# Own buffers for scaled weights, a key block's scores moved, transposes grouped, a last store in halves

## The chip, the cores and the metric

The kernel runs on one core of a Trainium2 chip. The metric is the time of one execution on the device in microseconds, taken as the median of several runs; lower is better.

## The reference

Three parts follow each other, all in fp32: attention over 4 x 12 heads of 448 tokens and 64 columns (scores capped by a tanh, softmax), a gated layer with two matmuls behind it, and a SoLU layer with a norm and a last matmul.

```python
scores = cap * np.tanh(scale * np.matmul(q, k.transpose(0, 1, 3, 2)) / cap)
attn = np.exp(scores - max); attn = attn / (attn.sum(-1) + 1e-09)
x = (attn @ v).transpose(0, 2, 1, 3).reshape(1792, 768)
h = ((x @ w1) * (x @ w2)) @ w3 @ w_out          # (1792, 768)
h = h @ w_in                                    # (1792, 1024)
solu = h * softmax(h)
ln = (solu - mean(solu)) / np.sqrt(var(solu) + 1e-06) * g_ln
out = ln @ moe2_w_out                           # (1792, 768)
```

(`max`, `mean` and `var` go along the last axis.) All weights come in as float64 and are turned into fp32 on the chip.

## The kernel before, in words

Every large product is made of three matmuls on operands split into a high and a low fp32r part (`THREE`). The kernel has these stages.

**Attention with the fold beside it** (0 to about 435 us). 24 pairs of heads are worked on in 12 groups `g` of three phases. Keys are cut in four chunks: three full ones for each head of the pair, and a fourth, the last keys, in which both heads' last 64 keys lie together. `scores` (L237 to L251) writes the scores of a chunk to a PSUM tile `sc0` or `sc1` (two banks each), `exps` (L257, L258) runs tanh in place and then exp to `p` on ScalarE, `split_scores` (L269 to L273) makes `hi` and `lo`, and `values` (L290) sums into the banks `o`. The first four pairs (`PLAIN`) skip the split of the scores. Beside this, `fold` multiplies w3 by w_out (L378) and the result by w_in (L396), once for all tokens, in two PSUM banks of tag `f`. From about 270 us on the gated products `ab` (L604) run beside the last heads, with `a` copied by ScalarE (L608) and `abs` multiplied on VectorE (L612).

**The queue of weights.** `Ahead` holds a list of pieces to be loaded, converted and split; `step` does the `rest` of the piece before and the `first` of the next. Loads go three ahead into `ld` (tag `ld`, 3 buffers, L159 or L161). `convert` turns a float64 piece into fp32 with three VectorE instructions (L168 to L170) in a buffer of tag `cv` (2 buffers). For most weights `split` then reads it (ScalarE L174, VectorE L175). For the last weights (`plan_last`, L529) ScalarE multiplies the `cv` buffer in place by g_ln (L535), and SyncE stores it to `wg_dr` (L536); 16 such pieces are stored between 359 and 467 us, the last four of them after the attention.

**The gated products alone** (about 435 to 580 us): `products` takes two PSUM tiles per weight block and batch, 36 matmuls into the two. Beside it `plan_sums` (L494 to L497) makes sums and differences of weight quarters in tiles `t` (tag `ts`) and stores them (L499).

**Seven-product blocks** (580 us to the end): 14 blocks, seven for the first matrix and seven for the last, each of seven products of 12 matmuls (L766) for a 2 x 2 block scheme. `seven` (L761) runs products 1, 2, 6, 7, 5, 4, 3; `kept` copies three of the partial sums from PSUM to SBUF (`p1`, `u2`, `p7`; L770), and VectorE adds them (L777, L786, L789); product 6 goes on in the bank that `p1` was copied from. The last part is copied by ScalarE (L791). Between the blocks `solu` does the row-wise part and stores it to `c_dr`; `turned` (L831) transposes the loaded tiles on TensorE (L836) into four banks `tp`, a quarter each time that `seven` calls `other`. The results go out in stores of 128 x 768 (L903).

**Order.** The program's instructions are put in order on each engine at build time, by a schedule that works with priorities and estimated times; `tc.high_priority` and `tc.issue_after` steer it. At run time each engine works strictly in its order.

**The start.** `load_pair(0)` loads q, k and v of the first pair (L197, L202), then `ahead.loads()` the first three weight pieces. 12 products of a zero tile (L663) run ahead of the first scores, and six more (L701) behind the scores of chunk 1. `ready[0]` takes pair 0 unsplit.

Of the kernel before, what the change touches and what calls it, by code (L numbers as in the profile page):

```python
# [38 lines left out]
WARM = 12  # L39
# [11 lines left out]
class Ahead:  # L51
# [9 lines left out]
    def loads(self):  # L61
        while self.loaded < len(self.items) and self.loaded < self.at + self.depth:
            _, load, _, _, _, there = self.items[self.loaded]
            if there is not None and not there():
                return
            load()
            self.loaded += 1

# [30 lines left out]
def attention_moe_solu(ctx: ExitStack, tc: tile.TileContext, q, k, v, cap, w12, w3t, wo, win, wout2, g_ln, out):  # L99
# [89 lines left out]
    def load_pair(n):  # L189
# [6 lines left out]
        for t, src in ((qd, q), (kd, k)):  # L196
            sync.dma_start(out=t, in_=src[n])  # L197
        if n in PLAIN:
            vd = at.tile([P, 2, S], F32, tag="lo", bufs=4, name=f"vf{n}").rearrange("p a b -> p (a b)")
            vd = vd[:, :NV * (D + 1)].rearrange("p (c d) -> p c d", c=NV)  # L200
            pool.memset(vd[:, :, D:], 1.0)
            sync.dma_start(out=vd[:, :, :D], in_=v[n])  # L202
        else:
            vd = at.tile([P, NV, D], F32, tag="vd", name=f"vd{n}")
            sync.dma_start(out=vd, in_=v[n])
# [31 lines left out]
    def scores(n, c, place_):  # L237

        qh, ql, kh, kl = ready[n][:4]
        sc = ps.tile([P, 2, HALF], F32, tag=f"sc{place_}", name=f"sc{n}_{c}")  # L240
# [246 lines left out]
    def plan_sums(kind, dr, t_dr, i_, part, n):  # L487
# [3 lines left out]
        def rest():  # L491
            b = lands.pop(i).rearrange("p (g h n) -> p g h n", g=2, h=2)
            t = [place["ts"].tile([P, HALF], F32, tag="ts", bufs=6, name=f"t{i}_{m}")[:, :2 * n].rearrange("p (t n) -> p t n", t=2) for m in range(2)]
# [35 lines left out]
    def plan_last(f):  # L529
        for u in range(2):  # L530
            i = len(ahead.items)

            def rest(i=i, u=u):
                t = cvs.pop(i)
                act.activation(t, t, AF.Copy, scale=gt[:, f:f + 1])  # L535
                sync.dma_start(out=wg_dr[f, u], in_=t)  # L536
            ahead.add(("g", f, u), lambda i=i, u=u: landing(i, wout2[f, u].bitcast(U32), DM, U32), lambda i=i: convert(i, DM // 2), rest)
# [118 lines left out]
    load_pair(0)  # L656
# [32 lines left out]
    for g in range(NP // 2):  # L689
        n, first, at_once = 2 * g, g % 2, 2 * g in PLAIN  # L690
        for phase in range(3):
# [6 lines left out]
            if not g and not phase:  # L698
                with tc.issue_after(tiled[0].ins):
                    for i in range(WARM // 2):  # L700
                        pe.matmul(idle[:, :S], zero[:, 0, :P], zero[:, 0], start=True, stop=True)  # L701
# [6 lines left out]
            for turn, x in enumerate((run[0], (n + phase, 3), run[1])):  # L708
                if turn == 1:
                    if phase == 2:  # L710
                        continue
                    with tc.high_priority():
                        sc = scores(*x, one)
                else:
                    sc = tiles[turn // 2]
# [45 lines left out]
    def seven(n, a, wb, w, c1, c2, other):  # L761
# [6 lines left out]
        def kept(bank, name):  # L768
            t = hp.tile([P, HALF], F32, tag="kept", bufs=3, name=f"{name}_{n}")[:, :w]
# [21 lines left out]
        act.copy(c1[:, w:], u)  # L791
# [39 lines left out]
    def turned(n, tps, q):  # L831

        tps[q] = ps.tile([P, HALF], F32, tag="tp", bufs=4, name=f"tp{n}_{q}")
        for i in range(4):
            f = 4 * (q // 2) + i
            pe.transpose(tps[q][:, i * P:(i + 1) * P], lands[f"c{2 * n + q % 2}"][:, f * P:(f + 1) * P], ident)  # L836
# [41 lines left out]
    for n in range(PAIRS):  # L878
# [4 lines left out]
        seven(n, a, ws, HALF, h1, h2, lambda q: turned(0, tps, q) if last else None)  # L883
# [14 lines left out]
    for n in range(PAIRS):  # L898
        tps, last = {}, n + 1 == PAIRS
        o1, o2 = (hp.tile([P, DF], F32, tag="h", bufs=4, name=f"o{t}")[:, :DM] for t in (2 * n, 2 * n + 1))  # L900
        seven(PAIRS + n, a, wg, w, o1, o2, lambda q: None if last else turned(n + 1, tps, q))
        for t, o in ((2 * n + 1, o2), (2 * n, o1)):
            sync.dma_start(out=out[t * P:(t + 1) * P, :], in_=o)  # L903
# [60 lines left out]
```

## Time and profile before

| | us |
|---|---|
| median of 3 runs | 836.03 |
| lowest, highest | 836.0, 838.24 |
| the profiled execution, its own time | 837.27 |
| its span, first to last instruction | 835.5 |
| TensorE busy with matmuls (PE) | 819.0 |
| VectorE (DVE) busy | 586.2 |
| ScalarE (ACT) busy | 478.4 |

A profile shows one execution. PE is TensorE's matmuls, PEld its weight loads, DVE is VectorE, ACT ScalarE, POOL GpSimd, SP SyncE, which issues most DMAs. L604 is line 604 of the kernel. An instruction's names are "out<-in". A wait is the idle time of an engine before an instruction, with what ended it. The ends of matmuls are modelled, so busy time of PE contains overlap.

### The profile page before, as it was taken

What the parts mean: (1) busy time and instruction counts of PE and PEld (TensorE: products, weight loads), DVE (VectorE), ACT (ScalarE), POOL (GpSimd) and SP (SyncE); (2) the same over time, 40 slices, a digit from 0 to 9 for tenths busy, and PEclk for the clock granted to TensorE, in tenths of its full rate; (3) what the DMA queues carried; (4) which work ended last, traced back from release to release, by engine and by line L of the source; (5) the groups of instructions that cost most, each with busy time, mean ns of one, the idle gap of its engine ahead of it and who ended that gap; (6) DMA issues with size and microseconds to landing.
All of it is one profiled execution on the core that took longest, in us unless ns stands there. A gap on an engine that the chain in (4) does not pass through costs nothing.

```text
span 835.5 us, 12215 instructions
## 1 busy us (share of the span) xinstructions
PE 819.0 (98%) x4363; PEld 682.9 (82%) x4363; DVE 586.2 (70%) x1048; ACT 478.4 (57%) x739; POOL 74.8 (9%) x149
## 2 busy tenths in 40 slices
PE   8999999999999999999899999999999999999998
PEld 4657888866777888887779899998888888999997
DVE  6889968878875787778855452433987877995452
ACT  6767868778677877765752220212555656763341
POOL 1110110110311221111111000000000000000000
PEclk9999999999999999999999999999999999999999
DMA  7878645578977355688677999983533325844211
GB/s 239 273 240 275 209 150 157 175 222 280 277 263 206 114 183 184 207 269 274 198 232 259 347 381 346 360 287 102 184 113 115 100 101 186 264 156 152 89 64 75
DMA packets 95645, 173.48 MB, mean 208 GB/s; under 512 B 13280, under 2 KB 66272, under 8 KB 93536
## 3 DMA queue, kind: packets, MB, share of 16 engines
q1 hardware_dynamic: 90592, 161.51, 57.5%
q0 software_dynamic: 4992, 11.19, 5.4%
q8 instruction: 34, 0.56, 0.3%
q14 instruction: 27, 0.22, 0.1%
HBM read 116.40 MB, written 50.68 MB: 200 GB/s over the span
## 4 chain that ended last, share of the span: by engine, by line
PE 70%; DVE 11%; DMA 11%; ACT 4%; issue 3%; SPq 0%; POOL 0%; DVEq 0%; POOLq 0%; ACTq 0%
PE ab L604 20%; PE u L766 16%; PE v L766 8%; PE o L290 6%; PE f L396 6%; PE f L378 5%; PE y L766 4%; DMA wg_dr<-cv 3%; PE sc L249 3%; DVE cv L169 2%; DMA ld<-in_wo 2%; DVE cv L170 2%; PE tp L836 1%; DVE cv L168 1%; DVE lo L273 1%
## 5 line engine op out<-in xcount | busy, mean ns | idle before, releaser
L604 PE MATMUL ab<-xs,wt 128*128 128x448 f32 x1152 | 241.7, 366 | 2.5 <-DVE abs L612 1.6
L604 PEld LDWEIGHTS ab<-xs,wt 128*128 128x128 f32 x1152 | 216.0, 188 | 23.9 <-DVE abs L612 2.0
L257 ACT ACTIVATE sc<-sc,qscale 128x896 f32<-128x896 f32 (+1 forms) x96 | 84.9, 884 | 34.8 <-PE sc L249 26.4
L258 ACT ACTIVATE p<-sc,capt 128x896 f32<-128x896 f32 (+1 forms) x96 | 85.6, 916 | 1.5
L290 PE MATMUL o<-hi,v 128*66 128x448 f32 (+1 forms) x360 | 84.7, 371 | 0.8 <-ACT x L306 0.6
L766 PE MATMUL u<-ws,a 128*128 128x512 f32 x336 | 82.1, 394 | 0.0
L378 PEld LDWEIGHTS f<-w,w_o 128*128 128x128 f32 x576 | 72.7, 191 | 10.5 <-issue 5.9
L378 PE MATMUL f<-w,w_o 128*128 128x256 f32 x576 | 78.5, 289 | 1.4 <-DVE w_o L175 0.9
L766 PEld LDWEIGHTS u<-ws,a 128*128 128x128 f32 x336 | 62.8, 187 | 14.8
L273 DVE TENSOR_TENSOR lo<-p,hi 128x896 fp32r<-128x896 f32 x60 | 64.9, 1084 | 9.7 <-ACT hi L269 9.5
L396 PE MATMUL f<-w_i,w 128*128 128x512 f32 x288 | 70.2, 393 | 1.1 <-DVE w L175 0.8
L608 ACT COPY a<-ab 128x448 f32<-128x448 f32 x32 | 17.0, 532 | 88.4 <-PE ab L604 84.1
L766 PE MATMUL u<-wg,c 128*128 128x384 f32 x336 | 65.4, 340 | 0.0
L396 PEld LDWEIGHTS f<-w_i,w 128*128 128x128 f32 x288 | 53.7, 188 | 14.3 <-DVE w L175 1.2
L168 DVE TENSOR_SCALAR cv<-ld 128x512 uint32<-128x512 uint32 (+1 forms) x80 | 32.8, 413 | 41.8 <-DMA wg_dr<-cv 25.3
L290 PEld LDWEIGHTS o<-hi,v 128*66 128x66 f32 (+1 forms) x360 | 39.1, 135 | 26.1 <-issue 9.1
L766 PEld LDWEIGHTS u<-wg,c 128*128 128x128 f32 x336 | 58.3, 188 | 0.1
L269 ACT CAST hi<-p 128x896 fp32r<-128x896 f32 x60 | 56.6, 947 | 0.4
L612 DVE TENSOR_TENSOR abs<-ab,a 128x448 f32<-128x448 f32 x32 | 19.9, 621 | 48.5 <-PE ab L604 41.3
L169 DVE SCALAR_TENSOR_TENSOR cv<-ld,cv 128x512 uint32<-128x512 uint32 (+1 forms) x80 | 52.1, 659 | 0.8
L170 DVE SCALAR_TENSOR_TENSOR cv<-ld,cv 128x512 uint32<-128x512 uint32 (+1 forms) x80 | 52.1, 658 | 0.7
L290 PE MATMUL o<-lo,v 128*66 128x448 f32 x120 | 42.6, 367 | 2.4 <-DVE lo L273 2.3
(132 smaller groups left out, 1237.4 us busy)
## 6 DMA issues: line engine op xcount, KB each, us to landing
ld<-in_w SPq DMA_DIRECT2D x24, 512.0 KB, 4.3
w_dr<-wt SPq DMA_DIRECT2D x8, 1536.0 KB, 6.5
wt<-w_dr SPq DMA_DIRECT2D x8, 1536.0 KB, 8.8
ld<-in_w3t SPq DMA_DIRECT2D x16, 512.0 KB, 4.4
ab_dr<-abs SPq DMA_DIRECT2D x32, 224.0 KB, 4.9
ldab<-ab_dr SPq DMA_DIRECT2D x14, 512.0 KB, 3.9
c_dr<-e SPq DMA_DIRECT2D x14, 512.0 KB, 2.6
ldc<-c_dr SPq DMA_DIRECT2D x14, 512.0 KB, 3.6
```

The source lines that it names most:

```text
L168: dve.tensor_scalar(x, hi, 5, 2, ALU.logical_shift_left, ALU.logical_shift_right)
L169: dve.scalar_tensor_tensor(x, hi, 0xC0000000, x, ALU.bitwise_and, ALU.bitwise_or)
L170: dve.scalar_tensor_tensor(x, lo, 29, x, ALU.logical_shift_right, ALU.bitwise_or)
L257: act.activation(sc[:, :w, :S], sc[:, :w, :S], AF.Tanh, scale=qscale)
L258: exp_[n, c] = act.activation(p, sc[:, :w, :S], AF.Exp, scale=capt)
L269: act.copy(hi, p)
L273: dve.tensor_tensor(lo, p, raw(hi), ALU.subtract)
L290: product_.append(pe.matmul(outs[n, j][:v_.shape[-1], :S], v_, t[rows, j if c < 3 else 0], **flags))
L378: pe.matmul(f[:, :QW], lw[:, a], rw[:, e], start=(g == 0 and m == 0), stop=(g == NF - 1 and m == 2))
L396: pe.matmul(f, w34[:, a, c, :], rw[:, e], start=(c == 0 and m == 0), stop=(c == NC - 1 and m == 2))
L604: pe.matmul(pp[f, b, i][:, :S], w[:, u], xs[b, c][:, e], start=(c == 0 and m == 0), stop=(c == NC - 1 and m == 2))
L766: pe.matmul(bank, a[m][:, x, k * P:(k + 1) * P], wb[m][:, e, k, :], start=(first and k == 0 and i == 0), stop=(k == NF // 2 - 1 and i == 2 ...
```

## The change

- `plan_last`: the scaled piece goes to a tile of its own, tag `wg`, 2 buffers; `cv` is no longer written in place. To make room, `ts` has 5 buffers for 6 and `kept` 2 for 3.
- Start: ten zero products, all ahead of the first scores; none behind them. The first weight load is issued between the loads of k and v of pair 0. In the first phase the scores of the last keys go to a bank of tag `f`, and their turn (exp and values) comes after chunk 1.
- `seven` calls `other` once, after product 6, and `turned` then does all 16 transposes.
- The last block: the last copy is shared by ScalarE and VectorE, and each result tile is stored in two halves.

```diff
@@ constants @@
-WARM = 12
+WARM = 10
@@ class Ahead @@
+    def first(self):
+        self.items[0][1]()
+        self.loaded = 1
@@ load_pair @@
-    def load_pair(n):
+    def load_pair(n, between=lambda: None):
         for t, src in ((qd, q), (kd, k)):
             sync.dma_start(out=t, in_=src[n])
+        between()
@@ scores @@
-        sc = ps.tile([P, 2, HALF], F32, tag=f"sc{place_}", name=f"sc{n}_{c}")
+        if place_ is None:
+            sc = ps.tile([P, HALF], F32, tag="f", bufs=2, name=f"sc{n}_{c}").rearrange("p (a s) -> p a s", a=1)
+        else:
+            sc = ps.tile([P, 2, HALF], F32, tag=f"sc{place_}", name=f"sc{n}_{c}")
@@ plan_sums: tag="ts" @@
-bufs=6
+bufs=5
@@ plan_last @@
-                t = cvs.pop(i)
-                act.activation(t, t, AF.Copy, scale=gt[:, f:f + 1])
+                t = conv.tile([P, DM // 2], F32, tag="wg", bufs=2, name=f"wg{f}_{u}")
+                act.activation(t, cvs.pop(i), AF.Copy, scale=gt[:, f:f + 1])
                 sync.dma_start(out=wg_dr[f, u], in_=t)
@@ start @@
-    load_pair(0)
+    load_pair(0, ahead.first)
@@ phases @@
-            if not g and not phase:
-                with tc.issue_after(tiled[0].ins):
-                    for i in range(WARM // 2):
-                        pe.matmul(idle[:, :S], zero[:, 0, :P], zero[:, 0], start=True, stop=True)
-            for turn, x in enumerate((run[0], (n + phase, 3), run[1])):
-                if turn == 1:
-                    if phase == 2:
-                        continue
-                    with tc.high_priority():
-                        sc = scores(*x, one)
-                else:
-                    sc = tiles[turn // 2]
+            turns = [(run[0], tiles[0]), ((n + phase, 3), None), (run[1], tiles[1])]
+            if phase == 2:
+                turns.pop(1)
+            elif not g and not phase:
+                turns[1:] = turns[:0:-1]
+            for x, sc in turns:
+                if sc is None:
+                    with tc.high_priority(), tc.issue_after(tiled[0].ins) if not (g or phase) else nullcontext():
+                        sc = scores(*x, one if g or phase else None)
                 split_scores(*x, exps(*x, sc))
@@ seven: tag="kept" @@
-bufs=3
+bufs=2
@@ seven @@
         dve.tensor_tensor(c1[:, :w], y, p1, ALU.add)
-        other(0)
         product(u, 6, False)
         u2 = kept(u, "u2")
-        other(1)
+        other()
         product(v, 7, True)
         p7 = kept(v, "p7")
-        other(2)
         product(u, 5, False)
         dve.tensor_tensor(c2[:, w:], u, p7, ALU.add)
-        other(3)
...
-        act.copy(c1[:, w:], u)
+        if last:
+            act.copy(c1[:, w:w + w // 2], u[:, :w // 2])
+            dve.tensor_copy(c1[:, w + w // 2:], u[:, w // 2:])
+        else:
+            act.copy(c1[:, w:], u)
@@ turned @@
-    def turned(n, tps, q):
+    def turned(n, tps):
+        for q in range(4):
...
@@ last blocks @@
-            sync.dma_start(out=out[t * P:(t + 1) * P, :], in_=o)
+            for part in (slice(0, w), slice(w, DM)) if last else (slice(0, DM),):
+                sync.dma_start(out=out[t * P:(t + 1) * P, part], in_=o[:, part])
```

## Rows read from the trace of the kernel before

**Rows 1.** The page's first part: busy us (share of the span) and instructions by engine.

```profile
PE 819.0 (98%) x4363; PEld 682.9 (82%) x4363; DVE 586.2 (70%) x1048; ACT 478.4 (57%) x739; POOL 74.8 (9%) x149
```

**Rows 2.** Busy time by stretch: length, then PE, PEld, DVE, ACT, POOL busy, PEclk, DMA share, GB/s.

```profile
358.00:440.00 82.00, 76.85 (x404) 62.13 (x403) 58.33 (x108) 53.11 (x78) 10.20 (x19) 1.00 0.76 247
440.00:580.00 140.00, 139.50 (x683) 127.78 (x682) 63.24 (x128) 28.22 (x45) 3.41 (x8) 1.00 0.89 306
580.00:698.00 118.00, 118.00 (x510) 95.17 (x509) 95.06 (x175) 65.53 (x113) 7.62 (x10) 1.00 0.37 123
```

**Rows 3.** Waits of PE, 358 to 440 us: total us, times, longest us.

```profile
PE o L290 <- DVE lo L273: 2.3, 3, 1.4
PE ab L604 <- DVE abs L612: 1.6, 1, 1.6
```

**Rows 4.** Waits of DVE, 358 to 440 us.

```profile
DVE cv L168 <- DMA wg_dr<-cv: 15.6, 7, 2.8
```

**Rows 5.** Timeline of DVE: start, us, instruction, in brackets the idle time before it.

```profile
377.14 0.43 DVE L168 TENSOR_SCALAR cv<-ld 128x512 uint32<-128x512 uint32 x1 [1.82 <-DMA wg_dr<-cv]
377.49 1.08 DVE L273 TENSOR_TENSOR lo<-p,hi 128x896 fp32r<-128x896 f32 x1
...
395.62 0.36 DVE L168 TENSOR_SCALAR cv<-ld 128x384 uint32<-128x384 uint32 x1 [2.22 <-DMA wg_dr<-cv]
...
401.47 0.43 DVE L168 TENSOR_SCALAR cv<-ld 128x512 uint32<-128x512 uint32 x1 [2.65 <-DMA wg_dr<-cv]
...
406.27 0.62 DVE L612 TENSOR_TENSOR abs<-ab,a 128x448 f32<-128x448 f32 x1
```

**Rows 6.** Timeline of ACT, 386 to 410 us.

```profile
397.20 0.62 ACT L535 ACTIVATE cv<-cv,gt 128x384 f32<-128x384 f32 x1 [4.14 <-DVE cv L170]
```

**Rows 7.** DMA issues, 358 to 440 us: count, KB each, median us to landing.

```profile
wg_dr<-cv SPq DMA_DIRECT2D x12, 192.0 KB, 5.0
```

**Rows 8.** Timeline of PE, 0 to 13 us.

```profile
1.39 4.78 PE L663 MATMUL idle<-zero 128*128 128x448 f32 x12 [1.39 <-DVE zero L660]
6.11 1.77 PE L249 MATMUL sc<-qd,kd 64*128 64x448 f32 x8
7.81 1.50 PE L701 MATMUL idle<-zero 128*128 128x448 f32 x6
...
12.54 0.65 PE L249 MATMUL sc<-qd,kd 64*128 64x448 f32 x2 [0.76 <-ACT p L258]
```

**Rows 9.** The first load of the keys: issue (ns, first and last start), and its landing.

```profile
L197 SPq DMA_DIRECT2D kd<-in_k x1: 424/424/424, 1.6 to 1.6; - x1
...
DMA to landing us min/median/max: 3.6/3.6/3.6
```

**Rows 10.** Timeline of ACT, 0 to 13 us.

```profile
10.31 0.61 ACT L257 ACTIVATE sc<-sc,qscale 128x448 f32<-128x448 f32 x1 [0.24 <-PE sc L245]
```

**Rows 11.** Timeline of PE, 816 to 836 us: the last product.

```profile
829.37 2.24 PE L766 MATMUL u<-wg,c 128*128 128x384 f32 x12
```

**Rows 12.** Timeline of ACT, 822 to 836 us: the last copy.

```profile
831.65 0.48 ACT L791 COPY o<-u 128x384 f32<-128x384 f32 x1 [5.77 <-PE u L766]
```

**Rows 13.** The stores of the output, 384 KB each.

```profile
DMA to landing us min/median/max: 2.3/2.3/3.1
```

**Rows 14.** The page's DMA issues: count, KB each, median us to landing.

```profile
c_dr<-e SPq DMA_DIRECT2D x14, 512.0 KB, 2.6
```

**Rows 15.** Timeline of PE, 805 to 812 us: eight transposes together.

```profile
809.68 1.04 PE L836 MATMUL tp<-ident,ldc 128*128 128x128 f32 x8
810.47 1.84 PE L766 MATMUL u<-wg,c 128*128 128x384 f32 x9
```

**Rows 16.** The stores of the sums (tile t).

```profile
DMA to landing us min/median/max: 4.2/6.2/11.7
```

**Rows 17.** Timeline of ACT, 631 to 646 us.

```profile
633.74 0.58 ACT L770 COPY p<-u 128x512 f32<-128x512 f32 x1
```

**Rows 18.** Timeline of DVE, 636 to 646 us.

```profile
640.85 0.69 DVE L789 TENSOR_TENSOR h<-v,u 128x512 f32<-128x512 f32 x1 [0.73 <-PE v L766]
```

More of the change, by code (lines that the diff above doesn't have):

```diff
@@ L492, in rest @@
             b = lands.pop(i).rearrange("p (g h n) -> p g h n", g=2, h=2)
-            t = [place["ts"].tile([P, HALF], F32, tag="ts", bufs=6, name=f"t{i}_{m}")[:, :2 * n].rearrange("p (t n) -> p t n", t=2) for m in range(2)]
+            t = [place["ts"].tile([P, HALF], F32, tag="ts", bufs=5, name=f"t{i}_{m}")[:, :2 * n].rearrange("p (t n) -> p t n", t=2) for m in range(2)]
             dve.tensor_tensor(t[0][:, 0], b[:, 0, 1], b[:, 0, 0], ALU.subtract)
@@ L759, in attention_moe_solu, with seven @@
     PAIRS = NTT // 2
-    def seven(n, a, wb, w, c1, c2, other):
+    def seven(n, a, wb, w, c1, c2, other, last=False):
         def product(bank, m, first):
@@ L768, in kept @@
         def kept(bank, name):
-            t = hp.tile([P, HALF], F32, tag="kept", bufs=3, name=f"{name}_{n}")[:, :w]
+            t = hp.tile([P, HALF], F32, tag="kept", bufs=2, name=f"{name}_{n}")[:, :w]
             act.copy(t, bank)
@@ L829, in solu @@
         sync.dma_start(out=c_dr[t], in_=e)
-    def turned(n, tps, q):
[L833 to L836, printed above, removed]
+    def turned(n, tps):
+        for q in range(4):
+            tps[q] = ps.tile([P, HALF], F32, tag="tp", bufs=4, name=f"tp{n}_{q}")
+            for i in range(4):
+                f = 4 * (q // 2) + i
+                pe.transpose(tps[q][:, i * P:(i + 1) * P], lands[f"c{2 * n + q % 2}"][:, f * P:(f + 1) * P], ident)
     def turned_operands(n, tps):
@@ L882, in attention_moe_solu @@
         h1, h2 = (hp.tile([P, DF], F32, tag="h", bufs=4, name=f"h{t}") for t in (2 * n, 2 * n + 1))
-        seven(n, a, ws, HALF, h1, h2, lambda q: turned(0, tps, q) if last else None)
+        seven(n, a, ws, HALF, h1, h2, lambda: turned(0, tps) if last else None)
         if not last:
@@ L900, in attention_moe_solu @@
         o1, o2 = (hp.tile([P, DF], F32, tag="h", bufs=4, name=f"o{t}")[:, :DM] for t in (2 * n, 2 * n + 1))
-        seven(PAIRS + n, a, wg, w, o1, o2, lambda q: None if last else turned(n + 1, tps, q))
+        seven(PAIRS + n, a, wg, w, o1, o2, lambda: None if last else turned(n + 1, tps), last)
         for t, o in ((2 * n + 1, o2), (2 * n, o1)):
-            sync.dma_start(out=out[t * P:(t + 1) * P, :], in_=o)
+            for part in (slice(0, w), slice(w, DM)) if last else (slice(0, DM),):
+                sync.dma_start(out=out[t * P:(t + 1) * P, part], in_=o[:, part])
         if not last:
```

## The prediction

> **What bounds the kernel now.** I read the page's busy times first, then the busy times by stretch, then who waits for whom inside the one stretch where TensorE loses time, then the rows of that stretch, and last the first 13 us and the end. TensorE (PE) is the bound: busy 819.0 us of 835.5 [rows 1]. Where it stands still can be seen by stretch [rows 2]: in 580 to 698 us it is busy 118.00 of 118.00, in 440 to 580 us 139.50 of 140.00, but in 358 to 440 us only 76.85 of 82.00. So 5.15 us are lost there, by a view whose matmul ends are modelled; it rather understates the loss. What comes behind (440 to 698 us) is dense, so time won before 440 us ends up in the total one for one, unless a new wait takes it.
>
> Who makes PE wait in that stretch [rows 3]: `lo` of L273 on VectorE (2.3 us in 3 waits) and `abs` of L612 on VectorE (1.6 us), together 3.9 of the 5.15. Why VectorE is late [rows 4]: it stood 15.6 us, in 7 waits, for stores `wg_dr<-cv` to land. These are the stores of the scaled last weights: `convert` (L168 to L170) writes one of two `cv` buffers, ScalarE scales it in place (L535), SyncE stores it (L536), and the convert after next needs the buffer back. VectorE works in order, so all behind that convert waits too. Two places show it [rows 5]: a convert begins at 377.14 after 1.82 us of waiting, and `lo` directly behind it at 377.49; converts begin at 395.62 and at 401.47 after 2.22 and 2.65 us, and `abs` comes only at 406.27, after the work that piled up. ScalarE in turn waited 4.14 us until 397.20 for a converted piece to scale [rows 6].
>
> **The change part by part.** Times are against the profiled execution (span 835.5, its own time 837.27 us); that one stands 1.24 us above the median of 836.03, and I take the differences off the median.
>
> *Own `wg` buffers.* L535 now writes a `wg` tile (2 buffers), so `cv` is free once ScalarE has scaled it (0.62 us [rows 6]) and not once the store has landed. Removed: VectorE's 15.6 us of waits. Added: ScalarE's third scaling must wait until the first one's store has landed, and behind it on ScalarE are queued the tanh and exp of the next scores, for which PE waits. How long is that? The store is issued right after its scaling and lands 5.0 us later [rows 7]. VectorE's wait for that same landing ended at 395.62 [rows 5]; convert's three steps then took 1.6 us, and the third scaling began at 397.20 [rows 6]. In the new kernel the convert runs before and the scaling can begin at about 395.6: of ScalarE's 4.14 us some 1.6 go and 2.5 stay. So the part of PE's loss that VectorE caused should go (2.3 + 1.6 = 3.9), and the 1.25 us that hang on ScalarE stay. I take 3.9; the ends are 0 (the wait only changes engine) and 5.15 (all of it). Next late are the loads of the weights, three buffers deep, which this stretch's converts would then catch up with.
>
> The Trainium skill, "DMA: Bandwidth & Descriptors", section "Anatomy of one DMA — SWDGE (gpsimd) path", gives about 2.0 us plus the bytes at 436 GB/s for one DMA; for 192 KB that is an estimate of 2.45 us, half of what the trace shows here (5.0). By the page the first store would have landed before the third scaling is due, and the first rival below would be the forecast; the row speaks for a wait that stays in part.
>
> *The start.* Twelve zero products run from 1.39 to 6.11, 0.39 us each, then the first scores; six more run from 7.81 for 1.50 us; behind them come the scores of the last keys, which had to wait until chunk 0's bank was read; later PE waits 0.76 us until 12.54 for chunk 1's exp [rows 8]. With ten, the first score can begin at 1.39 + 10 x 0.39 = 5.3. Its keys are issued at 1.6 and land 3.6 us later, at 5.2 to 5.3 [rows 9], so that is just possible: 0.75 us. The zero products' 0.39 us against 0.25 us for the later six [rows 8] are the lower clock (1.2 GHz) first and the higher one (2.4 GHz) later; if the first scores fall on the lower clock, up to half of their 1.70 us is added, so this step is worth 0.75 at best and -0.1 at worst; I take 0.45. The scores of the last keys now go into a bank of the fold and need no wait, so the values of chunk 0, queued behind them, can start when the exp of chunk 0 is done. On ScalarE the last keys' tanh (0.61 us [rows 10]) and exp (about as much) stood ahead of chunk 1's exp; in the new order they come behind it, and the scores at 12.54 can start 1.1 us earlier. But pair 1's split on VectorE, which the scores after those need, hardly moves. I take 1.0 us for the whole start; ends -0.5 and 1.6. Issuing the first weight load ahead of `v` brings it one issue forward on SyncE (0.42 us for the keys' [rows 9]), puts `v` behind 512 KB, and is covered: `v` is first needed after the first exp. Without that cover it would cost one such transfer, some 2 us at the 247 GB/s of [rows 2].
>
> *The end.* The last copy takes 0.48 us on ScalarE [rows 12]; halved between two engines about 0.3. The last store of 384 KB lands in 2.3 us [rows 13], one of 512 KB in 2.6 [rows 14], so one of 192 KB in about 1.9 (an estimate). Together 0.6; I take 0.5, as the halves queue behind each other on SyncE; ends 0.2 and 0.6.
>
> *Grouped transposes.* Where eight stood together they pushed the next product by 0.79 us, 0.10 each [rows 15], and 16 a block remain 16: the array's time is the same but for what the changes between kinds cost. They come after product 6 for all four tiles, earlier than two of them did, with four more products of the block (2.24 us each [rows 11]) in which to split their results. Nothing; ends -0.2 and +0.4 us of gain.
>
> *What pays for the buffers.* `ts` goes from 6 to 5: the second sums of a piece wait for the store of the piece two before; those stores land in 4.2 to 11.7 us [rows 16], and L612 is queued behind on VectorE. Yet a product's bank is needed again only a whole product pair later (36 matmuls of 140 us / 683 = 0.2 us [rows 2], 7.4 us), and VectorE is busy 63 of 140 us there [rows 2]. `kept` goes from 3 to 2: the copy `p1` of the next block then needs the buffer that L789 of this block frees. In the trace `p1` is copied at 633.74 [rows 17], and that L789 runs at 640.85 [rows 18], so the copy will be over 7 us later; product 6 of the next block adds to the copied bank and must wait for it, but product 3 of this block (12 matmuls; 2.24 us with 384 columns [rows 11], so about 3 us with 512) can run first. 0.2 us for both; ends 0 and several us (below).
>
> **Sum:** -3.9 - 1.0 - 0.5 + 0.2 = -5.2, so 836.03 - 5.2 = 830.8 us (832.1 for an execution like the profiled one).
>
> **The rivals.** *All of it goes:* stores land fast enough that ScalarE never waits. For it: the earlier converts spread the work. Against: the stores' 5.0 us [rows 7]. 836.03 - 5.15 - 1.6 - 0.6 - 0.3 = 828.4.
> *The wait moves to ScalarE:* the order on ScalarE stays, tanh and exp stand behind the waiting scaling, and of the delay only 1.6 of 4.14 us goes. For it: ScalarE's wait until 397.20 [rows 6]. Against: PE's named waits are VectorE's [rows 3]. 3.9 x 1.6/4.14 = 1.5, with 0.4 at the start and 0.5 at the end, less 0.2: 833.8.
> *Slower, by `kept`:* if product 6 of the next block is put right behind product 4 of this one, it waits for L789 (0.69 us [rows 18]) and the copy (0.58 us [rows 17]), 1.3 us. This decides from the point where less than 1.3 us of other products lies between the two. At half of that for 13 borders of 14 blocks, 8.5 us: 836.03 - 5.4 + 8.5 = 839.1. Against: VectorE ran L789 after 0.73 us without work [rows 18], so it is not late there, and the copy is short.
>
> **How the numbers follow.** Forecast 0.56 (own range 828.5 to 833.5), all of it 0.13, ScalarE 0.23, slower 0.08. The range reaches down over the first rival's half and up over the second's: 827.5 to 836.0. Of this kernel a measurement can tell about 0.3%, 2.5 us, from no change. Faster by more: most of the forecast (0.52), the first rival (0.13) and a part of the second (0.09), 0.74. Within: 0.19. Slower: 0.07.
>
> **What would show it.** Right: in 358 to 440 us no wait of L168 for `wg_dr`, PE's loss under 2 us, some waits of L535 for `wg_dr` on ScalarE; first score near 5.4; no PE waits in 580 to 698 us; last store's landing 0.5 us nearer to the last product. Wrong: ScalarE idle before L535 as long as VectorE was; PE waits at product 6 for `p1`; VectorE waits before L496 with PE waiting for `abs`; scores at the start on the lower clock.

## The result, and the profile after

The changed kernel takes 842.63 us (median of 9 runs, 839.63 to 846.77), the kernel before 836.52 on the same chip; the ratio is 1.0069, with a 95% interval of 1.0049 to 1.0089. By that ratio it is slower by 5.8 us, where 5.2 less were forecast. The profiled execution took 844.54 us, 1.9 above the median.

Lines of the code have moved by 4 to 8: L249 is now L257, L604 is L612, L535 is L543. First the page's first part of the changed kernel (before: [rows 1]), then its busy time by stretch (columns as in [rows 2]); the last three stretches are those in which the granted clock is at its lower level.

```profile
PE 821.4 (97%) x4355; PEld 684.0 (81%) x4355; DVE 587.9 (70%) x1049; ACT 476.7 (57%) x739; POOL 74.8 (9%) x149
```

```profile
14.00:60.00 46.00, 44.59 (x234) 27.27 (x234) 42.04 (x80) 31.34 (x49) 6.77 (x12) 0.96 0.78 250
60.00:84.00 24.00, 21.68 (x137) 15.60 (x136) 20.70 (x39) 16.57 (x25) 1.56 (x3) 1.00 0.83 252
358.00:440.00 82.00, 78.84 (x408) 63.80 (x407) 60.91 (x113) 53.93 (x79) 10.29 (x19) 0.98 0.74 248
440.00:580.00 140.00, 135.80 (x655) 123.84 (x654) 60.24 (x125) 27.21 (x44) 3.40 (x8) 0.99 0.88 305
580.00:698.00 118.00, 118.00 (x515) 95.93 (x514) 93.47 (x168) 64.57 (x111) 6.83 (x8) 1.00 0.35 116
...
420.70:424.10 3.40, 3.40 (x11) 3.00 (x10) 2.35 (x5) 3.37 (x6) 0.41 (x1) 0.50 0.89 272
475.30:478.70 3.40, 3.24 (x9) 2.92 (x10) 1.15 (x1) 0.00 (x0) 0.00 (x0) 0.50 0.99 415
14.50:17.90 3.40, 3.40 (x8) 0.76 (x4) 3.40 (x8) 0.27 (x2) 0.00 (x0) 0.50 0.11 45
```

PE is as busy as before in 580 to 698 us, but lost 4.2 us in 440 to 580, where it had lost 0.5 [rows 2]. In 358 to 440 us it lost 3.2 instead of 5.15. Three times the clock falls to 1.2 GHz (0.50) for 3.4 us, which can cost up to 1.7 us each (half of 3.4); in the profile of before it stood at 2.4 GHz from 5.96 us to the end.

Set beside each other matmul by matmul, the two traces give the place of each loss. The first score starts 0.9 us earlier than before and the first product of the values 1.2 us earlier; at 100 us the changed kernel is 2.7 us behind; at the end of attention 1.8; at 500 us 7.6, and so to the end, where 0.36 come back. So there are two losses: one in the first 80 us, one at about 470.

The waits of PE in the changed kernel (total us, times, longest) from 0 to 110 us, then in 358 to 440 (before: [rows 3]), then in 440 to 580:

```profile
PE sc L257 <- DVE kh L223: 1.9, 1, 1.9
PE f L386 <- DVE w L179: 1.8, 2, 1.2
...
PE o L298 <- DMA vf<-in_v: 1.0, 1, 1.0
...
PE o L298 <- DVE lo L281: 2.1, 1, 2.1
...
PE ab L612 <- DMA wt<-w_dr: 4.2, 1, 4.2
```

Each of the three falls of the clock stands beside such a wait: two come 1.1 and 0.4 us behind it, and the third begins at 475.32, in the last moment of the wait of 4.2 us, which ends at 475.46. At the start PE waits 1.01 us for v and 1.85 for pair 1's split; the clock falls at 14.53. Timeline of PE (before: [rows 8]):

```profile
5.23 1.77 PE L257 MATMUL sc<-qd,kd 64*128 64x448 f32 x8 [0.23 <-DMA kd<-in_k]
...
8.96 1.69 PE L298 MATMUL o<-p,vf 128*65 128x448 f32 x4 [1.01 <-DMA vf<-in_v]
...
13.45 0.47 PE L257 MATMUL sc<-ql,kh 64*128 64x448 f32 x2 [1.85 <-DVE kh L223]
```

The second loss begins on SyncE (SPq): the loads of the second pass's weight blocks (`wt<-w_dr`, 1.5 MB) and of the sums (`ld<-w_dr`) stand in one queue. Its timeline in the kernel before, then in the changed one:

```profile
449.27 2.53 SPq L159 DMA_DIRECT2D ld<-w_dr  x2
...
452.58 2.92 SPq L159 DMA_DIRECT2D ld<-w_dr  x2
...
461.53 0.32 SPq L429 DMA_DIRECT2D wt<-w_dr  x1
...
465.05 1.23 SPq L159 DMA_DIRECT2D ld<-w_dr  x2
```

```profile
451.19 3.07 SPq L163 DMA_DIRECT2D ld<-w_dr  x2
...
455.03 0.52 SPq L163 DMA_DIRECT2D ld<-w_dr  x1
...
457.80 5.44 SPq L163 DMA_DIRECT2D ld<-w_dr  x3
...
463.98 0.38 SPq L437 DMA_DIRECT2D wt<-w_dr  x1
```

Before, four of the sums' loads went ahead of the block's load and two behind it; now all six go ahead, and the block is issued 2.5 us later. Its landing, in the kernel before and in the changed one:

```profile
DMA to landing us min/median/max: 7.6/7.6/7.6
```

```profile
DMA to landing us min/median/max: 11.4/11.4/11.4
```

What had kept the last two back was the very wait that the change removes. VectorE's waits in the kernel before, 440 to 480 us:

```profile
DVE cv L168 <- DMA wg_dr<-cv: 9.6, 2, 7.8
```

While VectorE stood there, the `ld` buffers that it was to read stayed taken, and SyncE could not issue the next loads. Timeline of VectorE in the kernel before:

```profile
463.07 0.36 DVE L168 TENSOR_SCALAR cv<-ld 128x384 uint32<-128x384 uint32 x1 [7.82 <-DMA wg_dr<-cv]
...
464.47 0.56 DVE L170 SCALAR_TENSOR_TENSOR cv<-ld,cv 128x384 uint32<-128x384 uint32 x1
```

The convert behind the wait is done at 465.03, and SyncE issues the last two loads at 465.05, behind the block. The Trainium skill, "DMA: Bandwidth & Descriptors", section "Queues, rings and completion order", says that each DMA engine takes a ring's descriptors in ring order; the landing of 11.4 us for a load that was issued right behind the last three of the six, against 7.6 for one issued 6 us after the last of four, agrees.

### The profile page after: what moved, and what is told of

Its sections match the earlier page's. It is cut to its first block, busy times and chain, and to the rows that moved or that the text cites. A ratio compares the mean times of both kernels' runs of the same rounds, so it can differ in the third digit from the quotient of the medians.

```text
span 842.8 us, 12203 instructions
## 1 busy us (share of the span) xinstructions
PE 821.4 (97%) x4355; PEld 684.0 (81%) x4355; DVE 587.9 (70%) x1049; ACT 476.7 (57%) x739; POOL 74.8 (9%) x149
## 4 chain that ended last, share of the span: by engine, by line
PE 68%; DMA 15%; DVE 10%; issue 3%; ACT 3%; SPq 1%; POOL 0%; DVEq 0%; ACTq 0%; POOLq 0%
PE ab L612 18%; PE u L771 16%; PE v L771 8%; PE o L298 7%; PE f L404 5%; PE f L386 5%; PE y L771 4%; PE sc L257 3%; DMA ld<-in_w 2%; DVE cv L173 2%; DVE cv L174 2%; DMA inv<-x 2%; DMA ab_dr<-abs 2%; PE tp L843 1%; DMA ld<-in_wout 1%
## 5 line engine op out<-in xcount | busy, mean ns | idle before, releaser
L612 PE MATMUL ab<-xs,wt 128*128 128x448 f32 x1152 | 245.3, 370 | 4.6 <-DMA wt<-w_dr 4.2
L612 PEld LDWEIGHTS ab<-xs,wt 128*128 128x128 f32 x1152 | 218.6, 190 | 27.0 <-issue 4.6
L281 DVE TENSOR_TENSOR lo<-p,hi 128x896 fp32r<-128x896 f32 x60 | 65.0, 1085 | 12.1 <-ACT hi L277 11.8
L771 PE MATMUL u<-wg,c 128*128 128x384 f32 x336 | 63.3, 337 | 0.0
```

What stands on the lines that cost most here:

```text
L281: dve.tensor_tensor(lo, p, raw(hi), ALU.subtract)
L612: pe.matmul(pp[f, b, i][:, :S], w[:, u], xs[b, c][:, e], start=(c == 0 and m == 0), stop=(c == NC - 1 and m == 2))
L771: pe.matmul(bank, a[m][:, x, k * P:(k + 1) * P], wb[m][:, e, k, :], start=(first and k == 0 and i == 0), stop=(k == NF // 2 - 1 and i == 2 ...
```

## The experiments

All are measured against the kernel before on the same chip, in turns. The differences in the text below are the ratio less one, times 837 us; the column "us" has each run's own median, and the runs were on several chips. "Held" means that the sums' loads are held back, as in e4. "Start" is all that the change does in the first phase; the parts are named as in the change.

| run | what | us | ratio, 95% interval |
|---|---|---|---|
| e1_start | before + start | 842.03 | 1.0051 (1.0021, 1.0080) |
| e2_wg | before + wg, ts, kept | 837.27 | 0.9981 (0.9951, 1.0011) |
| e3_zeros | after + six zero products | 841.82 | 1.0045 (1.0019, 1.0070) |
| e4_held | after + sums' loads held | 837.63 | 0.9992 (0.9967, 1.0018) |
| e5_load | before + load order | 838.06 | 0.9996 (0.9977, 1.0015) |
| e6_order | before + start less load order | 841.47 | 1.0042 (1.0022, 1.0062) |
| e7_rest_held | all but the start, held | 831.36 | 0.9927 (0.9896, 0.9958) |
| e8_tail | before + ts, kept, transposes, halves | 837.85 | 0.9982 (0.9964, 0.9999) |
| e9_zeros_gone | before + fewer zero products | 836.86 | 0.9984 (0.9962, 1.0006) |
| e10_turn | before + bank and turn | 837.54 | 0.9996 (0.9973, 1.0018) |
| e11_exp_first | e4 + first casts later | 836.11 | 0.9996 (0.9971, 1.0021) |
| e12_rest | all but the start | 835.49 | 0.9984 (0.9961, 1.0007) |
| e13_cast_behind | e4 + one cast later | 849.78 | 1.0144 (1.0095, 1.0193) |
| e14_rest_turn | e7 + bank and turn | 832.70 | 0.9937 (0.9917, 0.9957) |
| e15_order_behind | e6 + one cast later | 850.08 | 1.0141 (1.0087, 1.0196) |
| e16_twelve | e6 with 12 zero products | 837.34 | 0.9997 (0.9978, 1.0017) |
| e17_twelve_held | e4 with 12 zero products | 833.47 | 0.9949 (0.9926, 0.9972) |
| e18_after_twelve | after with 12 zero products | 837.36 | 1.0007 (0.9985, 1.0029) |

### Which part loses

**e1_start.** The kernel before, with the start's edits alone:

```diff
-WARM = 12
+WARM = 10
-    load_pair(0)
+    load_pair(0, ahead.first)
... (bank f, the turn, and no zero products behind the scores, as in the change)
```

> The kernel before with the start of the change alone (ten zero products and none behind the scores, the first weight load between k and v, the last keys' scores in a fold bank). Theory: the start loses what it won, since pair 1's split on VectorE is no earlier and TensorE stands idle at 8 to 9 and 11.6 to 13.4 us; with the zero products gone the granted clock falls to 0.5 near 14 us. About 2.5 us slower than before (839). Rival, the forecast's own step: 1 us faster (835.5), and the loss of the changed kernel comes from elsewhere.

4.3 us more: the start alone costs most of what the whole change costs, and more than either theory expected. The clock falls twice in its profile, at 14.83 and, for 6.8 us, at 69.44.

**e2_wg.** The kernel before, with the weights' buffers and what pays for them:

```diff
+                t = conv.tile([P, DM // 2], F32, tag="wg", bufs=2, name=f"wg{f}_{u}")
-                act.activation(t, t, AF.Copy, scale=gt[:, f:f + 1])
+                act.activation(t, cvs.pop(i), AF.Copy, scale=gt[:, f:f + 1])
-tag="ts", bufs=6
+tag="ts", bufs=5
-tag="kept", bufs=3
+tag="kept", bufs=2
```

> The kernel before with the own wg buffers (and ts 5, kept 2) alone. Theory: TensorE loses about 2 to 3 us less in 358 to 440 us, but the loads of the sums, freed by the earlier converts, are issued ahead of the second block's wt load near 464 us; that load takes about 11 us and TensorE waits some 4 us for it, with a fall of the granted clock behind it. Net 2 to 4 us slower than before (839). Rival: the wait near 467 us comes from the start's shift; then this kernel is 2 to 4 us faster (833).

No measurable difference: neither the 2 to 4 us more of the theory nor the 2 to 4 us less of the rival is there. The two stretches do behave as the theory has them. Busy time by stretch, and PE's waits in 358 to 580 us:

```profile
358.00:440.00 82.00, 81.59 (x434) 68.09 (x433) 63.07 (x119) 54.01 (x80) 10.91 (x20) 1.00 0.74 252
440.00:580.00 140.00, 136.99 (x673) 125.88 (x672) 58.55 (x116) 28.36 (x44) 2.70 (x7) 1.00 0.88 306
```

```profile
PE ab L604 <- DMA wt<-w_dr: 3.0, 1, 3.0
```

PE wins 4.7 us in the first stretch (81.59 against 76.85) and gives 2.5 back in the second. The wait for the weight block is there without the start's edits, so it does not come from the start's shift. The profiled execution (831.8) was the fastest of ten and the only one with the clock at 1.000; the other nine had 0.995 to 0.998, so the median keeps less.

**e3_zeros.** The changed kernel, with six zero products put back:

```diff
+            if not g and not phase:
+                with tc.issue_after(tiled[0].ins):
+                    for i in range(6):
+                        pe.matmul(idle[:, :S], zero[:, 0, :P], zero[:, 0], start=True, stop=True)
```

> The changed kernel with the six zero products put back, behind the scores of the last keys. Theory: they fill TensorE's hole at 8 to 9 us, the granted clock stays at 1.0 through 14 to 18 us, and 1.5 us come back (841). Rival: the hole at 11.6 to 13.4 us alone brings the clock down, and the time is that of the changed kernel (842.6).

The fall at 14.5 us is gone (clock 1.00 in that stretch), yet it is only 2.0 us better than the changed kernel, within the intervals of the two. So the lower clock at 14.5 us is not the main loss of the start. (This run keeps ten first zero products, and with them the order of instructions that is described below.)

**e4_held.** The changed kernel, with the last loads of the sums behind the load of the second pass's second weight block:

```diff
+    def behind_again(load):
+        with tc.issue_after(again[NF + 1].ins):
+            load()
-lambda: landing(i, four(dr, i_, part, n), 4 * n, F32)
+lambda: behind_again(lambda: landing(i, four(dr, i_, part, n), 4 * n, F32))
```

> The changed kernel with the loads of the sums queued on SyncE behind the second block's wt load. Theory: that load lands within 8 us of its issue, TensorE's wait of 4.2 us near 467 us goes to under 1 us and the clock fall at 475 us with it: 5 us faster than the changed kernel (837.5). Rival: the transfers are full there anyway, the load lands as late, and less than 1 us is won.

6.4 us less than the changed kernel by the ratios, 5.0 by the medians: as expected. Timeline of SPq, PE's waits in 440 to 580 us and the busy time of that stretch:

```profile
463.17 0.37 SPq L439 DMA_DIRECT2D wt<-w_dr  x1
463.59 0.53 SPq L163 DMA_DIRECT2D ld<-w_dr  x1
...
464.82 4.46 SPq L163 DMA_DIRECT2D ld<-w_dr  x5
```

```profile
PE ab L618 <- DMA wt<-w_dr: 0.7, 1, 0.7
```

```profile
440.00:580.00 140.00, 139.25 (x679) 127.03 (x678) 63.25 (x128) 28.58 (x45) 3.39 (x8) 1.00 0.87 306
```

With all six loads behind the block, it lands in 7.2 us again, PE's loss in the stretch is 0.75 us, near the 0.5 of before, and the clock does not fall there.

### The start taken apart

**e5_load** has the load order alone, **e6_order** the rest of the start:

```diff
e5:
-    load_pair(0)
+    load_pair(0, ahead.first)
e6:
-WARM = 12
+WARM = 10
... (bank f, the turn, and no zero products behind the scores)
```

> The kernel before, with one edit: the first weight load is issued between k's and v's first loads instead of behind v's. Theory A (the load order opens the hole): v lands near 8.8 us instead of 6.18 and k of pair 1 near 12.7 instead of 11.63; VectorE's split of pair 1 begins about 0.8 us later and TensorE stands about 1 to 2 us before the scores of pair 1, so a fall of the granted clock to 0.5 in the first 80 us and 1.5 to 3 us more. Theory B (the zero products and the turn order open it; the load alone is covered by the twelve zero products and the six behind them): no fall of the clock, 0 to 0.8 us more.

> The kernel before, with the start's other edits alone: ten zero products instead of twelve, none behind the scores, the last keys' scores in a bank of the fold and in the new turn; the first weight load stays behind v's. Theory A (the load order opens the hole): first score near 5.2, v at 6.2, pair 1's split begins near 11.2 as before, TensorE's stall ahead of pair 1's scores is under 1.2 us and the clock stays at 1.0: 1.0 us less than before at 75 us. Theory B (taking the zero products away opens it): the stall ahead of pair 1's scores stays near 1.8 us, the clock falls to 0.5 near 14 us, and the run loses 2 to 7 us as with the whole start.

The load order by itself costs nothing measurable, so theory A of e5 fell. The other edits cost 3.5 us with v landing at 6.2 as before: e6 came out as its theory B, with a wait of 1.35 us ahead of pair 1's scores and a fall of the clock at 14.96. Whether those two are the cause, the next runs tell.

**e9_zeros_gone** and **e10_turn** divide e6 once more:

```diff
e9:
-WARM = 12
+WARM = 10
-                    for i in range(WARM // 2):
... (no zero products behind the scores)
e10:
... (bank f and the turn; 12 and 6 zero products stay)
```

> The kernel before with ten zero products instead of twelve and none behind the scores; bank, turn and loads as before. ScalarE's program keeps exp of the third chunk ahead of the first weight casts, as in the kernel before. Theory A (the loss of the start comes from a weight cast that stands ahead of that exp on ScalarE only when zero products and turn are changed together): first score near 5.4, no idle stretch of ScalarE near 14 to 18 us, within 1 us of the kernel before at 100 us: 837 to 838.5. Theory B (TensorE without zero products loses its clock by itself): a fall to 0.5 in the first 20 us and 2 to 5 us more.

> The kernel before with the last keys' scores in a bank of the fold and in the new turn; all 18 zero products stay, loads as before. ScalarE's program keeps exp of the third chunk ahead of the first weight casts. Theory A (cast ahead of exp): no idle stretch of ScalarE of over 2 us near 14 to 18 us, within 1 us of the kernel before at 100 us: 837 to 838.5. Theory C (the new turn is by itself what costs): 4 to 5 us more at 100 us, as with the start's order alone.

Neither costs anything measurable alone; together they cost 3.5 us. In e9 PE stands still 1.36 us at 8.5 without a fall of the clock in the first 300 us. What the two do together can be seen in the order of the engines' instructions. To count what has moved, take the longest sequence that two traces have in the same order (by operation, names and shapes, buffer numbers left out); what is outside it stands in another place. Against the kernel before, that is in e9 0 instructions of PE, 3 of ScalarE and 1 of VectorE, in e10 4, 4 and 1, but in e6 40, 23 and 39. The order is set at build time from estimated times, and only the two edits together make it come out otherwise.

**e11_exp_first**, **e15_order_behind** and **e13_cast_behind.** What e6 has on ScalarE and neither e9 nor e10 has is a cast that waits 3.04 us for VectorE and stands ahead of the third chunk's exp. Timeline of ScalarE in e6:

```profile
13.18 0.97 ACT L260 ACTIVATE sc<-sc,qscale 128x896 f32<-128x896 f32 x1
17.19 0.62 ACT L174 CAST w<-cv 128x512 fp32r<-128x512 f32 x1 [3.04 <-DVE cv L170]
17.72 1.00 ACT L261 ACTIVATE p<-sc,capt 128x896 f32<-128x896 f32 x1
```

e11 moves the first casts behind that exp in e4's kernel; e15 and e13 move this one cast, in e6's and in e4's:

```diff
e11:
-with tc.issue_after(exp_[0, 1].ins) if not g else nullcontext():
+with tc.issue_after(exp_[0, 2].ins) if not g else nullcontext():
e15, e13:
+            with tc.issue_after(exp_[0, 2].ins) if i == 2 else nullcontext():
                 split(th, tl, cvs.pop(i))
```

> The changed kernel with the sums' loads held behind the second pass's second weight block, as in the run that held them, and one more edit: the first weight casts come behind the third chunk's exp instead of the second's. Theory A (cast ahead of exp): ScalarE's 3.1 us of idle time ahead of that cast is gone, exp of the third chunk ends near 15.7 instead of 19.4, and the run is 2 to 5 us faster than the held one: 833 to 836. Theory B (TensorE's standing still ahead of pair 1's scores and the fall at 14.5 are the cost): the fall stays and with it the time, 837 to 838.

> The kernel before with the start's order alone (ten zero products, none behind the scores, bank and turn), and one edit more: the first fold weight's cast on ScalarE must come behind the third chunk's exp. Theory (that cast is the cause): ScalarE's exp of the third chunk ends near 15 instead of 18.7, no more than 0.5 us behind the kernel before at 100 us instead of 4.5, and a time of 836.5 to 838.5 instead of the 841.47 of the start's order alone. Rival (the clock's fall and TensorE's stall ahead of pair 1's scores are the cause): the stall of 1.3 us stays, the clock falls near 14 us, 840 to 842.

> The changed kernel with the sums' loads held, and the first fold weight's cast behind the third chunk's exp on ScalarE. Theory (start and loads are the two losses, and the start's is that cast): 3 to 5 us less than the held kernel without it (837.63): 832.5 to 834.5, with the weight load ahead of v still opening 1 us of idle time at 8 to 9 us. Rival: as the held kernel, 837 to 838.

In e15 the exp starts at 14.04 instead of 17.72 and the clock does not fall near 14 us, as the theory had it, yet the time is 11.8 us above before, far outside both expectations; e13 is as slow, and e11 no different from e4 by the ratios. The edit of one cast moved 161 instructions of PE, 90 of ScalarE and 157 of VectorE against e6, and e11's edit 198, 73 and 117 against e4. One instruction can't be moved alone in this kernel, so these three say nothing clear on that cast. They do show that a moved order can cost much (e13, e15) or nothing (e11).

**e16_twelve, e17_twelve_held, e18_after_twelve** turn the question round and leave all edits in but two zero products:

```diff
-WARM = 10
+WARM = 12
```

With twelve, e16's order is that of the kernel before (2, 1 and 0 instructions elsewhere), although nothing keeps PE busy behind the scores. Likewise e18's is that of e12, which has all of the change but the start (2, 1 and 1 elsewhere), while the changed kernel's differs from e12's in 40, 26 and 52 places.

> The start's order alone (bank, turn, no zero products behind the scores) with twelve first zero products instead of ten; the engines' programs then stand in the order of the kernel before. Theory (the order is the cost): VectorE's wait for the pair's q near 71 us is 0.6 us or less instead of 2.4, TensorE as busy in 60 to 84 us as before, 837 to 838.5 instead of 841.47. Rival (no zero products, no clock): TensorE stands idle over 1 us before pair 1's scores as with ten, the clock falls to 0.5 behind it, 840 to 842.

> The whole change with twelve first zero products instead of ten, and the sums' loads held. Theory (order and held loads are the two losses): 831 to 833.5, as the kernels that keep the old start or its turn alone (831.36 and 832.70), against 837.63 with ten. Rival: 836 to 838.

> The changed kernel with one number put back: twelve first zero products instead of ten. Theory: the 5 us of the start go, the 4 us of the wait for the second pass's second weight block stay: 835 to 837.5, as the kernel without the start (835.49), against 842.63. Rival: 841 to 843.

e16 is equal to the kernel before (e6: 3.5 us more); e18 5.2 us better than the changed kernel, from which it differs by one number; e17 3.6 better than e4. All three as the theory of the order has it; e17 is at the upper end, 1.8 us above e7, and e18 is 1.9 above e12, and in both pairs the intervals overlap.

The clock as a rival cause can be bounded. The profiles of e17 and e18 still have the fall near 14.5 us behind a wait of PE (1.92 and 1.70 us), as the changed kernel has, and e18 still waits 0.92 us for v, yet they are the faster ones. Each execution's mean granted clock is on record too. One less that mean, times 837 us, is the most that the lower clock can have cost (an estimate); averaged over the executions it is 4.5 us in the changed kernel and 3.1 in e18, 1.1 in e6 and 0.6 in the kernel before beside it, 2.7 in e1 and 0.9 beside that. So by this estimate the clock can account for at most 1.4 of the 5.2 us between the changed kernel and e18, 0.5 of the 3.5 us of e6, and 1.8 of the 4.3 us of e1.

What the order does, in ScalarE's timeline of e16:

```profile
13.57 1.01 ACT L260 ACTIVATE sc<-sc,qscale 128x896 f32<-128x896 f32 x1
14.61 1.01 ACT L261 ACTIVATE p<-sc,capt 128x896 f32<-128x896 f32 x1
...
17.25 1.23 ACT L174 CAST w<-cv 128x512 fp32r<-128x512 f32 x2 [0.76 <-DVE cv L170]
```

The exp comes ahead of the cast. And 60 to 84 us, busy time and VectorE's longest wait for a pair's q, in the kernel before, in e6 and in e16:

```profile
60.00:84.00 24.00, 22.93 (x158) 18.73 (x158) 22.80 (x44) 18.62 (x29) 1.85 (x4) 1.00 0.85 273
```

```profile
60.00:84.00 24.00, 20.99 (x128) 14.74 (x127) 19.82 (x37) 15.59 (x25) 1.58 (x4) 1.00 0.83 251
...
DVE qh L218 <- DMA qd<-in_q: 2.4, 1, 2.4
```

```profile
60.00:84.00 24.00, 24.00 (x159) 18.82 (x160) 23.31 (x45) 19.17 (x29) 2.12 (x4) 1.00 0.83 269
...
DVE qh L218 <- DMA qd<-in_q: 0.5, 1, 0.5
```

VectorE has 22.80 us of work in these 24 us before the change. In e6's order it stands 2.4 us for a q that lands late for its place, and PE, which needs the weights and splits that VectorE makes, is busy 1.9 us less in this stretch alone. In the changed kernel this wait is 2.7 us. It is 1.6 to 2.7 us in the runs with a moved order (the changed kernel, e1, e3, e4, e6, e11, e15; in e13 it is 1.0) and 0.4 to 0.9 in all whose order at the start is the old one. Over 14 to 84 us PE is busy 67.5 us in the kernel before, 68.1 in e16 and 67.8 in e18, but 64.5 in e6 and 66.3 in the changed kernel; e17, with 66.3, is the exception. Ten zero products with the old order cost nothing measurable (e9), ten with the moved order cost 3.5 us (e6), and two more bring back order and time (e16, e18). So the moved order as a whole is shown to be the start's main loss; how much of it hangs on this wait, on that exp or on another place was not measured.

### The rest

**e8_tail** is the kernel before with the parts of the last stages; **e12_rest** the whole change without its start, **e7_rest_held** that with e4's edit, **e14_rest_turn** e7 with e10's:

```diff
e8:
... (ts, kept, grouped transposes, last halves; wg and start as before)
e12, e7:
-WARM = 10
+WARM = 12
-    load_pair(0, ahead.first)
+    load_pair(0)
... (turn, bank and zero products as before; e7 also e4's edit)
e14:
... (e7, and of the start bank f and the turn)
```

> The kernel before with ts and kept smaller, the transposes grouped and the last halves stored apart; weights and start as before. Theory: no wait of TensorE behind 580 us, the distances from the fold's last product to the last product the same within 0.3 us, the last landing 0.4 us nearer to the last product: 0.2 to 0.6 us less than before. Rival (fewer buffers cost waits in one stage and win nothing): 1 to 4 us more, with TensorE waits for the copy into kept or VectorE waits for stores of the sums.

> All of the change but its start, and the sums' loads not held: own wg buffers, smaller ts and kept, grouped transposes, last halves. Theory: the end of attention 5 to 6 us earlier than before, then 2 to 4 us given back in one wait for the second pass's second weight block, sometimes with a fall of the clock behind it; 833.5 to 837, and 3 to 5 us above the kernel that holds the loads (831.36). Rival (holding brings nothing by itself, and the 831 were the halves, the transposes and the weights): 830.5 to 832.

> All of the change but its start (own wg buffers, ts and kept smaller, transposes grouped, last halves), and the last six loads for the sums held behind the load of the second pass's second weight block. Theory (the start and the wait for that weight block are the two losses): TensorE has no wait for a weight block at 455 to 475 us, the clock stays at 1.0, the end of attention is 5 us earlier than before and the end 5 to 6.5: 830.5 to 832.5. Rival (the new waits of the seven-product stage for ts and kept, or the holding itself, take it back): 834 to 838 with TensorE waits behind 475 us.

> The rest of the change with the sums' loads held (831.36 before), and of the start the bank and the turn alone, all 18 zero products kept; ScalarE's program keeps that exp ahead of the cast. Theory: the turn brings at most the 0.7 us that its own run showed at 20 to 100 us: 830.5 to 832. Rival (the start's losses come with the turn): 834 to 836.

e8: 1.5 us less, at the edge of what the interval shows and more than expected, and no wait of PE behind 580 us. It scales in place in `cv` as before, and in its trace SyncE still issues four of the sums' loads ahead of the weight block and two behind it; so it is the weights' own buffers that set those two free, and not the smaller `ts` and `kept`. e12 and e7 differ by 4.8 us, e18 and e17 by 4.9: the loads' order twice more, with the old order of instructions. e7 is the fastest kernel of all, 6.1 us below the one before and 11.9 below the changed one. Its busy time by stretch and PE's wait in 440 to 580 us:

```profile
358.00:440.00 82.00, 81.48 (x432) 67.75 (x431) 62.45 (x118) 53.62 (x79) 10.85 (x20) 1.00 0.74 249
440.00:580.00 140.00, 138.64 (x680) 127.22 (x679) 59.92 (x118) 28.56 (x45) 2.70 (x7) 1.00 0.89 310
```

```profile
PE ab L610 <- DMA wt<-w_dr: 1.4, 1, 1.4
```

The wait for the weight block that e7's theory wanted gone is still 1.4 us. e14 shows that the turn adds nothing on top: the two intervals overlap.

## Why the prediction was wrong

**The weights' own buffers: right in their place.** The step gave 3.9 us with an upper end of 5.15. In 358 to 440 us e2 wins 4.7 and e7 4.6. The wait does move to ScalarE, as said, but there it costs PE next to nothing: of the 82 us PE is idle 0.4 in e2 and 0.5 in e7. ScalarE's waits in the changed kernel, 340 to 440 us (VectorE's before: [rows 4]):

```profile
ACT wg L543 <- DMA wg_dr<-wg: 10.9, 4, 3.7
```

So the 1.25 us that were to stay with ScalarE were too many, and the rival by which the wait only changes engine is out. "Next late are the loads of the weights" came true too. VectorE's timeline, and PE's behind it, in the changed kernel:

```profile
417.41 0.36 DVE L172 TENSOR_SCALAR cv<-ld 128x384 uint32<-128x384 uint32 x1 [2.52 <-DMA ld<-in_wout]
...
419.21 1.08 DVE L281 TENSOR_TENSOR lo<-p,hi 128x896 fp32r<-128x896 f32 x1
```

```profile
420.35 0.76 PE L298 MATMUL o<-lo,v 128*66 128x448 f32 x2 [2.08 <-DVE lo L281]
```

PE's wait at 420 us is there in the changed kernel, e3 and e4 (1.95 to 2.10 us), which have the moved order, and in none of e2, e7, e12, e14, e17 and e18. In the changed kernel it leaves PE's loss in the stretch at 3.2 us, where the text wanted under 2.

**"Time won before 440 us ends up in the total one for one, unless a new wait takes it": the first step that failed.** The half-sentence named the way out but gave it no price. VectorE's wait until a store had landed was also what kept two loads behind the weight block on SyncE's queue; with the wait gone they go ahead of it, and PE waits 4.2 us instead of 0.5, with a fall of the clock at its end. It costs 6.4 us by e4, 4.8 by e12 and e7 and 4.9 by e18 and e17, the clock included. The prediction asked who waits behind a new wait, and not which issues an old wait had held back. The rows of SPq in 440 to 470 us would have shown it: the block's load took 7.6 us, and PE had to wait 0.5 us for it even then.

**The start: the second step that failed, and the larger one.** The sum gave 1.0 us less, with 0.5 more as its worst end; measured alone, it costs 4.3 (e1), and in company 5.4 (e4 against e7) to 7.1 (the changed kernel against e12). The single pieces came out near the text: first score at 5.23 (5.3 forecast) and not slowed by the lower clock, the values 1.2 us earlier. Of these only "covered" was wrong: PE waits 1.01 us for v in the changed kernel. The step that failed is that only the moved instructions were priced, with the order of all others taken as it was. That order is made anew at each build, and here it came out worse for the three engines up to 84 us. Both parts alone leave it as it was and cost nothing measurable (e9, e10), and two more zero products bring it back (e16, e17, e18). "Pair 1's split hardly moves" was wrong where the weight load goes ahead of v: in the changed kernel the split begins at 12.01 instead of 11.22, behind two converts that begin later themselves. Which of the moved instructions costs most stays open: the one cast that was suspected could not be moved alone (e11, e13, e15).

**The end** gave 0.36 us of the 0.5. The last copies in the changed kernel, on ScalarE and VectorE (behind the last product, which starts at 837.00; before: [rows 11, 12]):

```profile
839.28 0.32 ACT L794 COPY o<-u 128x192 f32<-128x192 f32 x1 [5.77 <-PE u L771]
```

```profile
839.64 0.36 DVE L795 COPY o<-u 128x192 f32<-128x192 f32 x1 [1.88 <-ACT o L794]
```

They were to take about 0.3 side by side, but VectorE's begins when ScalarE's is done: 0.72 us, where one copy had taken 0.48 [rows 12]. What is won comes from the smaller stores: the last one lands in 1.9 us, as estimated, and the last before in 2.3. The Trainium skill, "PSUM — Partial Sum Buffer", section "PSUM bank collisions raise a hardware error", says that the compiler's scheduler sets a dependency between engines that touch one bank and quadrant, ScalarE and VectorE too; this row agrees with it.

**Transposes, ts and kept**: no loss, as forecast (0.2 us in the sum). PE is busy 118.00 of 118.00 us in 580 to 698 and has no wait behind 580 us, so the rival that came out slower, by `kept`, did not happen. VectorE does wait for stores of the sums, 5.2 us in two waits, but PE has no wait on VectorE in 440 to 580 us. The range's upper end, 836.0, stood on rivals of single waits; no rival had the build's order or the queue of loads in it. (In the first rival's sum the last term, 0.3 us, is read from no row.)

## What to carry to other kernels

A wait that is taken away also sets free what stood behind it: look on the DMA queue for loads that will now be issued earlier, and for a critical load behind them that has no slack (here PE had waited 0.5 us for it already). Where a schedule sets the order at build time, compare the instruction order of the engines before pricing an edit; two edits that are free alone can cost 3.5 us together, and a single number (twelve zero products or ten) can be worth 5. Of this change the part to keep is the weights' buffers with the sums' loads held behind the weight block, and the old start: 831.36 us.

## What the hardware showed beyond this

The granted clock fell in some executions of nearly every kernel, the one before among them, though not in the profile of that one. In the profiles a fall stands beside waits of PE, but the length of a wait alone does not tell: in e16 falls come behind waits of 0.92 (with one of 0.64 just before), 0.97 and 1.11 us (at 51.7, 195.1 and 434.0), in e2 a wait of 3.01 us at 465 brings none, and in e9 one of 1.36 us at 8.5 brings none either. The mean clock of single executions lies between 0.988 and 1.000, and it explains only a part of the spread of their times: all ten executions of e14 have 1.000 and take from 830.39 to 834.12 us, and in the nine of the changed kernel time and clock do not go together (846.77 us at 0.994, 840.11 at 0.993).
